# Batch 1's local attention heads in the transposed form and one slot earlier, with V loads and output buffers rearranged

## The chip, the cores and the metric

The kernel runs on one core of a Trainium2 chip. The metric is device time in microseconds (us) for one launch; the times shown are the median of several runs. A profile is of one execution, which has its own time; its span runs from the first to the last instruction.

## The reference

Sparse attention over 8 batches, 8 heads, 576 positions and head size 64, followed by a bilinear feed-forward layer:

```python
scores = scale * np.matmul(q, k.transpose(0, 1, 3, 2))
mask_local = (rel >= 0) & (rel < stride)                      # heads 0 to 3, stride 32
mask_strided = (rel >= 0) & (pos[None, :] % stride == pos[:, None] % stride)   # heads 4 to 7
attn = softmax(where(mask, scores, -1e9)); o = attn @ v
x = o.transpose(0, 2, 1, 3).reshape(B * S, H * D)             # 4608 x 512
out = ((x @ w_a) * (x @ w_b)) @ w_out                         # w_a, w_b: 512 x 1536; w_out: 1536 x 512
```

## The kernel before, in words

**Stages and slots.** The attention of batch 0 is written out by hand in a list (ORDER, L506). After it the kernel walks through 144 slots (L833): the feed-forward layer has 9 tiles of 512 tokens, and each tile has 16 slots. In slots 0 to 11 of a tile `ffn_ab` (L548) forms one block of 128 columns of x @ w_a and x @ w_b: eight matmuls at L545, a copy of the first result by ScalarE (L562), a product by VectorE into the tile `pf` (L565 or L567). In slots 12 to 15 the output is formed: for tiles 0, 1 and 2 by `ffn_y` (L692, twelve matmuls at L699, a copy by ScalarE at L705, a store by SyncE at L707, which the change calls plain outputs), for the later ones by `ffn_ys`. Slot numbers below count from the start, so slot 16 is the first of tile 1.

**Attention steps.** The attention of batches 1 to 7 is put between these matmuls. A unit `u` is a pair of heads (`c = u // 2`) and one half of the positions; units 0 to 3 are local heads, 4 to 7 strided ones. The steps are Tk and Tq (transposes of k and q by TensorE, batches 0 and 1 only), S (scores at L356, exponential by ScalarE at L364, mask by VectorE at L374), V (attention times V) and X (transposes of the result into `xT`, L479 and L495). The tables STEPS and LATER say behind which slot a step is issued; a position x.5 means in the middle of slot x + 1, after half of its matmuls. "V0(1)" below means step V of unit 0 of batch 1.

**Two forms of V.** Batches 0 and 1 use `V_p`, `V_r`, `V_n` (L383 to L433): the probabilities are the weights, V with one column of ones moves, so the output has positions on partitions and carries the sums; VectorE takes a reciprocal (L418) and multiplies (L433), and step X transposes. From batch `FIRST_D = 2` on, `step_VT` (L443) takes V and 64 columns of ones as the weights, and the probabilities move (L454): the output is already transposed and the sums lie on partitions 64 to 127. ScalarE takes the logarithm of the sums (L463) and the exponential of its negative (L464), and VectorE multiplies twice (L468 or L470), straight into `xT`. No X step is needed. The 64 columns of ones have to be in the V buffers before: `fill_v` (L109) writes them by a memset on GpSimd.

**Buffers and queues.** The V buffers `vl_buf` (local) and `vs_buf` (strided) are two each, used by batches of even and odd number. Each of the engines runs its own instructions in the order written; nothing is reordered by a scheduler. GpSimd (POOL) issues all loads from DRAM, one after another, through eight completion lanes: the load that takes a lane first waits until the load before it in that lane has landed. POOL also does memsets, and from slot 14 on a copy of one element (`pace`, L842) of the slot's result, which holds POOL's queue back to the slot whose loads come next. SyncE (SP) issues the stores of the outputs and, from batch 2 on, the copies from SBUF to SBUF that bring transposed k and q into place (L314, L318), issued by `step_D` (L292) behind transposes by VectorE (L299, L304). `do(i, f)` (L797) puts a piece of work behind slot i; the numbers `gs` (L811) say where the pieces of `step_D` go.

**Shared resources near the change.** PSUM has one buffer `o` for results of V after batch 0, one `st` for scores, one `tp` for transposes and three `mm`. The tile `y_sb` for plain outputs has two buffers, so the copy of output j waits for the store of output j - 2.

Of the kernel before, what the change touches and what calls it, by code (L numbers as in the profile page):

```python
# [7 lines left out]
F32 = mybir.dt.float32  # L8
# [6 lines left out]
FIRST_D = 2  # L15
# [15 lines left out]
def kernel(  # L31
# [10 lines left out]
    nc = tc.nc  # L42
    B, H, S, D = q.shape
    assert (B, H, S, D) == (8, 8, 576, 64)
    scale = 1.0 / (D ** 0.5)
    d_model = H * D
# [6 lines left out]
    HL = H // 2  # L53
# [6 lines left out]
    fsb = ctx.enter_context(tc.tile_pool(name="ffn", bufs=2))  # L60
# [21 lines left out]
    vl_buf = [const.tile([128, HL * 6, VW], BF16, name=f"vl{i}") for i in range(2)]  # L82
# [3 lines left out]
    vs_buf = [const.tile([NP, HL, RS, VW], BF16, name=f"vs{i}") for i in range(2)]  # L86
# [11 lines left out]
    def consts(i):  # L98
        if i == 0:
            for p in p_buf:  # L100
                nc.vector.memset(p[:, :, W:], 0.0)
        nc.vector.memset(kT_buf[i][0][:, :, 0:PAD], 0.0)
        nc.vector.memset(kT_buf[i][1], 0.0)
        nc.vector.memset(vl_buf[i][:, :, D:D + 1], 1.0)
        nc.vector.memset(vs_buf[i][:, :, :, D:D + 1], 1.0)
        if i == 0:
            nc.vector.memset(vl_buf[0][:PAD, 0, 0:D], 0.0)
# [44 lines left out]
    def spin(n):  # L152
        for _ in range(n):
            nc.tensor.matmul(cur["misc"][:, :224], lhsT=nc.const_aps.tensor(1.0, [128, 128], BF16),
                             rhs=nc.const_aps.tensor(1.0, [128, 224], BF16), start=True, stop=True)
# [58 lines left out]
    def load_vl(b, blocks=(0, HL * 6)):  # L214

        t = vl_buf[b % 2]
        f, e = blocks
        if (b, f) == (0, 0):
            f = 1
        src = bass.AP(tensor=v.tensor, offset=(b * H * S + LW * f - PAD) * D,  # L220
                      ap=[[D, 128], [LW * D, e - f], [1, D]])
        nc.gpsimd.dma_start(out=t[:, f:e, 0:D], in_=src)
# [17 lines left out]
    def load_w(c):  # L240
        f = slice(128 * WCH[c], 128 * WCH[c + 1])
        for src, dst in ((moe_w_a, wa_sb), (moe_w_b, wb_sb)):
            nc.gpsimd.dma_start(out=dst[:, :, f], in_=src.rearrange("(ko ki) f -> ki ko f", ki=128)[:, :, f])

    def load_wo(c):
        nc.gpsimd.dma_start(
            out=wo_sb[:, 3 * c:3 * (c + 1)],
            in_=moe_w_out.rearrange("(fo fi) d -> fi fo d", fi=128)[:, 3 * c:3 * (c + 1)],
        )
# [165 lines left out]
    def V_r(b, u):  # L415
        c, half, M, n, G = unit(u)
        rc = sb.tile([128, 2, 4], F32, tag="rc", name="rc")
        nc.vector.reciprocal(rc[:n, :, :G].unsqueeze(3), held[b, "o", u][1])  # L418
        held[b, "rc", u] = rc
# [13 lines left out]
        nc.vector.tensor_mul(dst, ov, rc[:n, :, :G].unsqueeze(3).to_broadcast([n, 2, G, D]))  # L433

    def step_V(b, u):
        if b >= FIRST_D:
            step_VT(b, u)
            return
        V_p(b, u)
        V_r(b, u)  # L440
        V_n(b, u)
# [55 lines left out]
    def step_X(b, c):  # L497
# [12 lines left out]
        F1b F1c""".split()  # L510


    STEPS = {1: {5: "Tk2", 5.5: "Tk3", 6: "Tq2", 7: "S4", 7.5: "Tq3", 8: "S5", 8.5: "V4", 9: "S6 Tk0", 9.5: "V5", 10: "S7 Tq0",
                 10.5: "V6", 11: "S0 Tk1", 11.5: "V7", 12: "Tq1 S1", 12.5: "V0 X2", 13: "S2", 13.5: "V1 X3 S3", 14: "V2",
                 14.5: "V3 X0", 15: "X1"},
             2: {20: "S0", 20.5: "S1", 21.5: "V0", 22: "S2", 23: "V1", 23.5: "S3", 24.5: "V2", 25: "S4", 26: "V3", 26.5: "S5",
                 27.5: "V4", 28: "S6", 28.5: "V5", 29: "S7", 29.5: "V6", 30: "V7"}}
    LATER = {-1: "S0", 0: "S1", 1: "V0", 2: "S2", 3: "V1", 4: "S3", 5: "V2", 6: "S4", 7: "V3", 8: "S5", 9: "V4", 10: "S6",
             11: "V5", 12: "S7", 12.5: "V6", 14: "V7"}
    FN = {"Tk": step_Tk, "Tq": step_Tq, "S": step_S, "V": step_V, "X": step_X}  # L520
# [10 lines left out]
    def mm_bank(shape):  # L531
        nm = "tp" if used[0] % 4 == 3 and used[0] >= 0 else "mm"
        used[0] += 1
        return psum4[nm].tile(shape, F32, tag=nm, name="mm")
# [50 lines left out]
    yst = {}  # L585
# [106 lines left out]
    def ffn_y(t, j, mid):  # L692
        pf = pfs[t]

        c0 = 0
        for z, n in enumerate((256, 128, 128) if (t, j) == (NT - 1, 3) else (d_model,)):
            y = mm_bank([128, n])
            for f in range(FD):
                nc.tensor.matmul(y, lhsT=pf[:, f, 128 * j:128 * (j + 1)], rhs=wo_sb[:, f, c0:c0 + n],  # L699
                                 start=(f == 0), stop=(f == FD - 1))  # L700
                if f == FD // 2 - 1:
                    mid()
            y_sb = fsb.tile([128, n], F32, tag="y_sb", name="y_sb", bufs=2)
            act = t < NT - 1 or (j + z) % 2 == 1
            (nc.scalar.copy if act else nc.vector.tensor_copy)(y_sb, y)  # L705
            r0 = TTOK * t + 128 * j
            (nc.scalar if z == 2 else nc.sync).dma_start(out=out[r0:r0 + 128, c0:c0 + n], in_=y_sb)  # L707
            c0 += n
        return y_sb[:1, :1]


    with tc.manual_schedule(engines={ENG.PE, ENG.SP, ENG.Pool, ENG.DVE, ENG.Activation}):
# [29 lines left out]
        for nm in ORDER:  # L742
            if nm[0] == "*":
                spin(int(nm[1:]))
            elif nm == "C0":
                for x, cp, n in ((raw[0], nc.vector.tensor_copy, "k"), (raw[1], nc.scalar.copy, "q")):
                    cp(nats[0, n, False][:, 0:2].rearrange("p h r d -> p (h r d)"), x[:96])
            elif nm == "C1":
                for p in (slice(PAD, 64), slice(64, 128)):
                    nc.vector.tensor_copy(vl_buf[0][p, 0, 0:D], raw[2][p, :D])  # L750
            elif nm == "M":
                mask_local2()
            elif nm[0] == "G":
                mask_group(int(nm[1]))
                if nm == "G1":
                    load_vs(0)
                    for c in range(2):
                        load_w(c)
                    load_w(2)
                    load_qk(1, True)  # L760
                    load_vs(1)
                    load_w(3)
                    load_qk(1, False)
                    load_w(4)
                    for c in range(4):
                        load_wo(c)
                    load_vl(1)
            elif nm == "Z":
                zero_qz(1, nc.scalar, ((0, 0),))
            elif nm[0] == "F":  # L770
                f = int(nm[1])
                if nm[2] == "a":
                    if f == 0:
                        ab = pst.tile([128, 2, 512], F32, tag="st", name="ab")
                        first[f] = [ab[:, 0], ab[:, 1]]
                    else:
                        first[f] = [psum4[x].tile([128, 512], F32, tag=x, name="ab") for x in ("misc", "o")]
                ab_mm(0, f, first[f], {"a": (0, 1), "b": (2,), "c": (3,)}[nm[2]])
            else:
                PART[nm[:-2] + nm[-1]](int(nm[-2]))  # L780
# [6 lines left out]
        for b in range(1, B):  # L787
            for pos, names in (STEPS.get(b) or {16 * (b - 1) + x: n for x, n in LATER.items()}).items():
                steps.setdefault(pos, []).append((b, names.split()))
# [7 lines left out]
        def do(i, fn, *args):  # L797
            at.setdefault(i, []).append(lambda: fn(*args))

        for b in range(FIRST_D, B):  # L800
            g0 = 16 * (b - 2)
            if b == FIRST_D:
                for g, fn, *a in ((0, load_qk, b, False), (1, load_qk, b, True), (3, load_vl, b), (6, load_vs, b)):
                    do(g0 + g, fn, *a)
            else:
                for h in range(HL):
                    do(g0 + h - (0 if b == FIRST_D + 1 else 2), load_qk, b, False, (h,))
                    do(g0 + h + (6 if b == FIRST_D + 1 else 2), load_qk, b, True, (h,))
                    do(g0 + h + 10, load_vs, b, (h,))
                do(g0 + (10 if b == FIRST_D + 1 else 7), load_vl, b)  # L810
            gs = {2: (14, 14, 14, 15, 16, 16, 17, 17, 18, 18), 3: (8, 9, 10, 11, 12, 13, 14, 15, 16, 17)}.get(b) or (  # L811
                3, 5, 7, 9, 12, 13, 14, 15, 16, 17)
            for (z, nm, part), g in zip(((0, "k", 0), (0, "k", 1), (0, "q", 0), (0, "q", 1), (1, "k", 0), (1, "k", 1),
                                         (1, "k", 2), (1, "q", 0), (1, "q", 1), (1, "q", 2)), gs):
                do(g0 + g, step_D, b, z, nm, part)
# [5 lines left out]
        for i, jz in ((2, (0, 0)), (3, (1, 0)), (0, (0, 1)), (5, (1, 1))):  # L821
            do(i, zero_qz, 0, nc.vector, (jz,))
        do(17, rezero, 1)
        for i, t in ((0, vl_buf[0]), (0, vs_buf[0]), (18, vl_buf[1]), (19, vs_buf[1])):
            do(i, fill_v, t)
        for n in range(5):
            for z in range(2):
                do(33 + 2 * n + z, fast_w, n, slice(3 * z, 3 * z + 3))
# [45 lines left out]
```

The softmax here doesn't subtract the row's maximum and nothing guards it: scores larger than these inputs give would overflow.

## Time and profile before

| | |
|---|---|
| median of 6 runs | 340.56 us (338.43 to 343.27) |
| the profiled execution | 338.43 us |
| its span | 336.3 us |
| TensorE matmuls busy | 323.6 us (96% of the span) |
| VectorE, ScalarE, GpSimd busy | 252.0, 202.2, 174.7 us |
| granted TensorE clock, mean | 0.995 |

The profiled execution is the fastest of the six; the rest of its time, 338.43 less 336.3, lies outside the span. PE's busy time overlaps: matmuls are pipelined, so the time that a matmul costs is the distance between the starts of two groups and not the duration in the row.

### The profile page before, as it was taken

How to read it: one execution, taken by the hardware profiler on the slowest of the kernel's cores; microseconds unless marked ns; L12 is line 12 of the kernel's file. 1: busy time of each engine (PE TensorE's matmuls, PEld its weight loads, DVE VectorE, ACT ScalarE, POOL GpSimd, SP SyncE). 2: the span in 40 equal slices, each digit the busy share in tenths (PEclk: the TensorE clock that was granted, in tenths of full speed). 3: DMA queues.
4: the chain of work that ended last, by engine and by line, in shares of the span. 5: the costliest groups of instructions: out<-in, count | busy, mean ns of one | idle time of the engine just before them, and what ended most of it. 6: DMA issues, size and time to landing. Idle time of an engine off the chain costs nothing.

```text
span 336.3 us, 7611 instructions
## 1 busy us (share of the span) xinstructions
PE 323.6 (96%) x2781; PEld 201.9 (60%) x2814; DVE 252.0 (75%) x475; ACT 202.2 (60%) x326; POOL 174.7 (52%) x293
## 2 busy tenths in 40 slices
PE   8999999999979999999999999999999999999992
PEld 6654555445535554556899985558555854674472
DVE  6867656758749984799999999999878744734561
ACT  5764855468758765787577756885678533223320
POOL 8934539899636644664577557843312031312132
PEclk9999999999999999999999999999999999999997
DMA  9999999998989699978898999899023022004004
GB/s 157 154 202 196 202 178 164 194 154 94 142 147 133 119 80 167 120 136 66 85 75 140 173 106 74 135 163 124 23 64 121 2 66 61 1 7 121 0 2 125
DMA packets 102446, 37.60 MB, mean 112 GB/s; under 512 B 77449, under 2 KB 98313, under 8 KB 102409
## 3 DMA queue, kind: packets, MB, share of 16 engines
q0 software_dynamic: 87760, 19.58, 64.8%
q1 hardware_dynamic: 14648, 17.53, 18.1%
q8 instruction: 22, 0.36, 0.4%
q14 instruction: 16, 0.12, 0.1%
HBM read 39.71 MB, written 9.44 MB: 146 GB/s over the span
## 4 chain that ended last, share of the span: by engine, by line
PE 68%; DMA 15%; POOL 6%; DVE 4%; issue 3%; ACT 1%; SPq 0%; DVEq 0%; ACTq 0%; POOLq 0%
PE mm L545 43%; PE mm L670 16%; DMA vl<-in_v_dram 4%; PE o L454 3%; DMA wa_sb<-in_moe_w_a_dram 3%; DMA shared<-in_k_dram 3%; PE st L356 3%; PE mm L699 3%; DMA qz10l<-tq 2%; DMA raw<-in_q_dram 1%; POOL vs L110 1%; POOL vl L110 1%; DMA natk<-in_k_dram 1%; DVE tq L299 1%; DMA out_dram<-y_sb 1%
## 5 line engine op out<-in xcount | busy, mean ns | idle before, releaser
L545 PE MATMUL mm<-xT,wa_sb 128*128 128x512 bf16 (+1 forms) x453 | 108.8, 357 | 1.5 <-DVE xT L470 0.6
L545 PE MATMUL mm<-xT,wb_sb 128*128 128x512 bf16 (+1 forms) x463 | 108.5, 357 | 0.3
L562 ACT COPY a_sb<-mm 128x512 f32<-128x512 f32 x106 | 62.1, 586 | 48.6 <-PE mm L545 46.4
L545 PEld LDWEIGHTS <-wb_sb 128*128 128x128 bf16 x480 | 46.4, 98 | 45.2 <-issue 1.5
L842 POOL CAST pace<-pf 1x1 f32<-1x1 bf16 x83 | 29.3, 353 | 82.5 <-DVE pf L565 73.7
L565 DVE TENSOR_TENSOR pf<-a_sb,mm 128x512 bf16<-128x512 f32 x72 | 48.5, 674 | 21.0 <-PE mm L545 17.9
L545 PEld LDWEIGHTS <-wa_sb 128*128 128x128 bf16 x480 | 42.6, 98 | 31.2
L364 ACT ACTIVATE p<-st 128x576 bf16<-128x576 f32 (+1 forms) x64 | 41.6, 650 | 10.1 <-PE st L356 9.5
L463 ACT ACTIVATE xr<-o 64x576 f32<-64x576 f32 x48 | 31.1, 647 | 24.8 <-PE o L454 24.5
L670 PEld LDWEIGHTS <-ps 128*128 128x128 bf16 x366 | 34.5, 98 | 5.3 <-DVE ps L578 1.2
L699 PE MATMUL mm<-wo_sb,pf 128*128 128x512 bf16 x140 | 33.7, 379 | 0.5 <-DMA wo_sb<-in_moe_w_out_dram 0.2
L464 ACT ACTIVATE xr<-xr 64x576 f32<-64x576 f32 x48 | 32.8, 683 | 1.5
L470 DVE TENSOR_TENSOR xT<-o,xr 64x288 bf16<-64x288 f32 x48 | 21.5, 448 | 14.8 <-ACT xr L464 13.8
L567 DVE TENSOR_TENSOR pf<-a_sb,mm 128x512 bf16<-128x512 f32 x34 | 22.9, 674 | 7.6 <-ACT a_sb L562 5.7
L468 DVE TENSOR_TENSOR xT<-o,xr 64x288 bf16<-64x288 f32 x48 | 21.5, 448 | 9.0 <-ACT xr L464 8.4
L670 PE MATMUL mm<-wf,ps 128*128 128x256 bf16 x210 | 26.3, 273 | 0.1
L374 DVE TENSOR_TENSOR p<-p,mask_l 128x576 int16<-128x576 int16 x32 | 19.4, 607 | 7.5 <-ACT p L364 7.5
L234 POOL DMA_DIRECT2D vs<-in_v_dram x24 | 19.5, 816 | 5.0 <-PE st L356 2.8
L699 PEld LDWEIGHTS <-pf 128*128 128x128 bf16 x144 | 12.9, 98 | 13.4 <-issue 0.5
L842 POOL COPY pace<-y_sb 1x1 f32<-1x1 f32 x18 | 3.4, 187 | 33.6 <-ACT y_sb L626 14.8
L210 POOL DMA_DIRECT2D ql<-in_q_dram x24 | 16.0, 665 | 7.1 <-DMA wo_sb<-in_moe_w_out_dram 3.7
L210 POOL DMA_DIRECT2D kl<-in_k_dram x24 | 16.0, 668 | 5.8 <-issue 3.5
(137 smaller groups left out, 479.5 us busy)
## 6 DMA issues: line engine op xcount, KB each, us to landing
out_dram<-y_sb SPq DMA_DIRECT2D x32, 256.0 KB
vl<-in_v_dram POOLq DMA_DIRECT2D x7, 384.0 KB, 8.9
kl<-in_k_dram POOLq DMA_DIRECT2D x24, 72.0 KB, 3.0
ql<-in_q_dram POOLq DMA_DIRECT2D x24, 72.0 KB, 3.2
vs<-in_v_dram POOLq DMA_DIRECT2D x24, 72.0 KB, 4.6
wo_sb<-in_moe_w_out_dram POOLq DMA_DIRECT2D x4, 384.0 KB, 11.4
natk<-in_k_dram POOLq DMA_DIRECT2D x20, 72.0 KB, 3.0
natq<-in_q_dram POOLq DMA_DIRECT2D x20, 72.0 KB, 3.2
```

The costliest lines, as they stand in the source:

```text
L210: nc.gpsimd.dma_start(out=t[32 * h:32 * h + 32], in_=src[b, h].rearrange("(i y) d -> y i d", y=32))
L364: nc.scalar.activation(p[:M, :, :W], st[:M, :, :W], ACT.Exp, scale=scale)
L463: nc.scalar.activation(r, sums, ACT.Ln)
L464: nc.scalar.activation(r, r, ACT.Exp, scale=-1.0)
L468: nc.vector.tensor_mul(dst[:, W * half:W * (half + 1)], o[:64, j, :W], r[:, j])
L545: nc.tensor.matmul(ps_[:, c0:c0 + n], lhsT=w[:, kk, 128 * f:128 * (f + 1)], rhs=xT[:, kk, x0:x0 + n], start=(kk == first and c0 == 0), sto ...
L562: nc.scalar.copy(a_sb, ab[0])
L565: nc.vector.tensor_mul(pf[:, f, :].rearrange("p (i a s) -> p a i s", i=2, s=16), halves(a_sb), halves(ab[1]))
L567: nc.vector.tensor_mul(pf[:, f, :], a_sb, ab[1])
L670: nc.tensor.matmul(dst, lhsT=lhs(g, q), rhs=rhs(g)[:, n], start=g == 0 and (tail and k == "7" or new and q == 0), stop=g == FG - 1, skip_g ...
L699: nc.tensor.matmul(y, lhsT=pf[:, f, 128 * j:128 * (j + 1)], rhs=wo_sb[:, f, c0:c0 + n], start=(f == 0), stop=(f == FD - 1))
L842: nc.gpsimd.tensor_copy(pace, done)
```

## The change

In four parts:

1. Units 0 to 3 of batch 1 (the local heads) use `step_VT`. Their steps X0 and X1 go. The steps of batch 1 are moved: V follows its S by about one slot instead of one and a half, V0(1) moves from the middle of slot 13 to the middle of slot 12, V3(1) stays in the middle of slot 15. The strided units 4 to 7 keep their form.
2. `vl_buf[1]` has to hold 64 columns of ones before batch 1, so the fills are moved to slot 0 (`vl_buf[1]`, `vl_buf[0]`, `vs_buf[0]`), and the loads of the last chunk of w_a and w_b, of w_out and of batch 1's local V are moved from ORDER to slot 0, between the fills. The order of the loads among themselves stays. The small memset of ones for `vl_buf[1]` on VectorE goes.
3. Batch 2's loads of V are issued behind slot 16 (local) and slots 18 to 21 (one strided head each) instead of slots 3 and 6, where POOL had issued them behind the loads of batch 2's k and q. The transposes of batch 2's local k go from slot 14 to slot 13, one of its local q from slot 15 to 14, one piece of its strided k from slot 16 to 15. V7(2) moves from behind slot 30 to the middle of slot 31.
4. A plain output takes half of a tile of 128 x 2 x 512: two outputs share a tile, and there are two tiles. The size of the tag in SBUF stays, since the later tiles' outputs use it in this size already.

```diff
-        nc.vector.memset(vl_buf[i][:, :, D:D + 1], 1.0)
+        if i == 0:
+            nc.vector.memset(vl_buf[i][:, :, D:D + 1], 1.0)
...
     def step_V(b, u):
-        if b >= FIRST_D:
+        if b >= FIRST_D or u < 4:
             step_VT(b, u)
             return
...
-    STEPS = {1: {5: "Tk2", 5.5: "Tk3", 6: "Tq2", 7: "S4", 7.5: "Tq3", 8: "S5", 8.5: "V4", 9: "S6 Tk0", 9.5: "V5", 10: "S7 Tq0",
-                 10.5: "V6", 11: "S0 Tk1", 11.5: "V7", 12: "Tq1 S1", 12.5: "V0 X2", 13: "S2", 13.5: "V1 X3 S3", 14: "V2",
-                 14.5: "V3 X0", 15: "X1"},
+    STEPS = {1: {5: "Tk2", 5.5: "Tk3", 6: "Tq2", 7: "S4", 7.5: "Tq3", 8: "V4 S5", 8.5: "Tk0", 9: "V5 S6", 9.5: "Tq0",
+                 10: "V6 S7", 10.5: "S0", 11: "V7 Tk1", 11.5: "V0 S1", 12: "Tq1", 12.5: "V1 S2", 13: "X2 S3", 13.5: "V2 X3",
+                 14.5: "V3"},
              2: {20: "S0", 20.5: "S1", 21.5: "V0", 22: "S2", 23: "V1", 23.5: "S3", 24.5: "V2", 25: "S4", 26: "V3", 26.5: "S5",
-                 27.5: "V4", 28: "S6", 28.5: "V5", 29: "S7", 29.5: "V6", 30: "V7"}}
+                 27.5: "V4", 28: "S6", 28.5: "V5", 29: "S7", 29.5: "V6", 30.5: "V7"}}
...
-            y_sb = fsb.tile([128, n], F32, tag="y_sb", name="y_sb", bufs=2)
+            if j % 2 == 0:
+                yst[t] = fsb.tile([128, 2, d_model], F32, tag="y_sb", name="y_sb", bufs=2)
+            y_sb = yst[t][:, j % 2, :n]
...
                     load_qk(1, False)
-                    load_w(4)
-                    for c in range(4):
-                        load_wo(c)
-                    load_vl(1)
...
+        do(0, fill_v, vl_buf[1])
+        do(0, load_w, 4)
+        do(0, fill_v, vl_buf[0])
+        for c in range(4):
+            do(0, load_wo, c)
+        do(0, load_vl, 1)
+        do(0, fill_v, vs_buf[0])
         for b in range(FIRST_D, B):
             g0 = 16 * (b - 2)
             if b == FIRST_D:
-                for g, fn, *a in ((0, load_qk, b, False), (1, load_qk, b, True), (3, load_vl, b), (6, load_vs, b)):
-                    do(g0 + g, fn, *a)
+                do(0, load_qk, b, False)
+                do(1, load_qk, b, True)
+                do(16, load_vl, b)
+                for h in range(HL):
+                    do(18 + h, load_vs, b, (h,))
...
-            gs = {2: (14, 14, 14, 15, 16, 16, 17, 17, 18, 18), 3: (8, 9, 10, 11, 12, 13, 14, 15, 16, 17)}.get(b) or (
+            gs = {2: (13, 13, 14, 14, 15, 16, 17, 17, 18, 18), 3: (8, 9, 10, 11, 12, 13, 14, 15, 16, 17)}.get(b) or (
...
-        for i, t in ((0, vl_buf[0]), (0, vs_buf[0]), (18, vl_buf[1]), (19, vs_buf[1])):
-            do(i, fill_v, t)
+        do(19, fill_v, vs_buf[1])
```

## The prediction

> **What bounds the kernel now.** I read the table by stages first: PE is busy 96% of the span, and from 104 us on it lacks under 1 us in each 30, so nothing there can be won but by fewer matmuls. The idle time that the change can touch lies before 104 us. The timeline of PE shows it, gap by gap (start, us, work, and in brackets the idle time before it and what ended it):
>
> ```profile
> 46.27 0.41 PE L410 MATMUL o<-vs,p 72*128 72x65 bf16 x8
> ...
> 47.53 0.81 PE L699 MATMUL mm<-wo_sb,pf 128*128 128x512 bf16 x3 [0.20 <-DMA wo_sb<-in_moe_w_out_dram]
> ...
> 50.21 0.35 PE L410 MATMUL o<-vl,p 128*128 128x65 bf16 x6
> ...
> 59.38 0.30 PE L479 MATMUL tp<-ident,xr 96*128 96x96 bf16 x3 [0.38 <-DVE xr L433]
> ...
> 69.04 0.22 PE L356 MATMUL st<-qz01l,kT0l 128*128 128x96 bf16 x1 [0.57 <-DMA qz01l<-tq]
> ...
> 94.04 0.43 PE L454 MATMUL o<-p,vs 72*128 72x72 bf16 x8 [1.10 <-DVE xT L470]
> ...
> 99.20 0.38 PE L545 MATMUL mm<-xT,wa_sb 128*128 128x512 bf16 x1 [0.59 <-DVE xT L470]
> ```
>
> The last two waits have one cause, seen on ScalarE: a plain output's copy waits for the store of two outputs before, and V7(2)'s logarithm stands behind it.
>
> ```profile
> 92.35 0.68 ACT L464 ACTIVATE xr<-xr 64x576 f32<-64x576 f32 x1
> 96.23 0.59 ACT L705 COPY y_sb<-mm 128x512 f32<-128x512 f32 x1 [3.20 <-DMA out_dram<-y_sb]
> 96.84 0.65 ACT L463 ACTIVATE xr<-o 64x576 f32<-64x576 f32 x1
> ```
>
> What no wait on PE shows is how close a transfer comes. The chain of waits in order of time has batch 1's local V:
>
> ```profile
> 35.74 0.93 issue
> 36.67 13.38 DMA vl<-in_v_dram
> 50.05 0.28 issue
> 50.33 0.66 POOL ql L210
> ```
>
> It lands at 50.05, and V0(1), its first user, starts on PE at 50.21: it fits by 0.16 us. So the row speaks against calling V0 sooner.
>
> **The change part by part.**
>
> **Work on PE.** Distances between starts: six matmuls of the old V take 0.18 us (55.50 to 55.68), of the new one 0.25 (72.14 to 72.39), an X of six 0.25 (57.16 to 57.41). Four V cost 4 x 0.07 = +0.28, two X save 0.50: -0.22. ScalarE gets four pairs of 0.65 + 0.68 and loses two copies of 0.64 (+4.0); VectorE gets eight multiplies of 0.45 and loses four pairs of 0.19 + 0.55 (+0.6). The two are busy 5.4 and 6.3 of the 9.3 us from 50.2 to 59.5, so it fits as a sum; the order is looked at below.
>
> **V0(1) one slot sooner.** The middle of slot 12, where V0(1) now stands, is where V7(1) stands in the trace: 46.27. It ends 0.25 later, so PE asks for `vl` at about 46.5. Slots 8 to 11 may cost up to 0.7 before that (V5 now stands one slot behind S5, and VectorE does the two instructions of V4, 0.2 + 0.7, ahead of S5's mask); the wait below swallows it. The load is not sooner: it stays behind the same loads of w and w_out, and its place in POOL is held by the lane (1.37 us idle before 36.67, for batch 1's k). The two fills ahead (1.40 us each by the row of the memset at 50.98) go into idle time of 1.48 us before 29.37 and, for the second, of 0.19 + 1.37 us before 36.67. w_out is issued 1.4 us later, but at 32.1 the loads of w ahead of it are still running (the last lands at 40.1), so the queue doesn't run dry. I leave the landing at 50.05, with 1 us to either side, as the mixing of w_out with `vl` isn't shown.
>
> Here the Trainium skill ("DMA: Bandwidth & Descriptors", section "Anatomy of one DMA") weighs the other way: a load from the GpSimd queue takes about 2.0 us plus its bytes over 436 GB/s. For 384 KB that is 2.9 us; `vl` would be there at 39.6, before 46.5, and this step would cost nothing. The row has 13.38 for this very load, behind a queue of w and w_out. I take the row.
>
> PE then goes from V0(1) at 50.13 by the new order: 4 V x 0.25, 3 S x 0.26, Tq1 0.38, 2 X x 0.25, seven halves of an output at 1.30 and slot 16 (1.73): 13.5 us. One new wait: Tq1 moves next to S2. ScalarE, after V0 (start to end of both activations 1.84 by 72.14 to 73.98), has S1's exponential (0.54), output 0's copy (0.48) and q's two copies (2 x 0.64): ready at 54.3, while PE wants S2's second matmul at 53.9; with 0.1 at S3 that is 0.5. V3's product is ready at 63.6 and slot 16 asks for that chunk of `xT` at 63.7: nothing. So slot 17 starts at 50.1 + 13.5 + 0.5 = 64.1, against 61.26 before (last matmul at 61.04 plus 0.22): **+2.85 us**. This already holds the -0.22 and the ends of the waits of 0.20 and 0.38. Bounds: +1.8 to +3.9, by the landing.
>
> **Batch 2's V loads behind the query transfers.** In 59.5 to 72.1 the queues are full (DMA share 1.96 by the table of stages), and S0(2) waits 0.57 us for q. With 3072 + 4 x 576 short rows gone from there, q is in place about 1 us sooner relative to S0(2): **-0.57** (0 to -0.57). What it risks: `vl` is issued behind slot 16's pace: 64.1, plus copy, product and pace, 1.5: at 65.6. V0(2) asks at 64.1 + 4 slots of 1.73 + S0 0.26 + 2.86 (69.26 to 72.14) = 74.2, that is 8.6 us later. The median from issue to landing is 8.9 for these loads (page), 5.5 to 14.0 with all nine; batch 2's own took 9.1 (58.46 to 67.60) behind eight loads that are now through. I take +0.1 here (0 to 5.4, weighed below). Moved past POOL's queue: the four strided heads (0.82 each, 3.3) now stand among batch 3's loads, the memset of `vl_buf[1]` (1.4) is gone from there, so batch 3's k and q are issued some 1.9 us later relative to PE. At slot 24 VectorE's first transpose of k ran at 79.01 with 0.43 us until the multiply behind it was due (80.15): I add +0.2 (0 to 1). The fill of `vs_buf[0]` (1.83) stands before k and q of batch 2, in time that POOL spent waiting for lanes (four times 1.2 us from 40.8 to 47.8).
>
> **Four half buffers, V7(2) half a slot later.** Output 2 of tile 1 now waits for stores of tile 0, done 25 us before. The 3.20 us on ScalarE go. V7(2) has the 1.30 us of six more matmuls between it and V6(2): its wait of 1.10 for `o` goes. Its product is then ready 2.65 us after its start (0.25 + 0.65 + 0.68 + 0.91 and handovers), and the chunk of `xT` is asked for after 0.25 + 1.30 + 0.26 + 1.30 = 3.1: the 0.59 goes too, with some 0.15 around it. **-1.8** (-0.5 to -1.9: S0(3) now comes 1.1 us sooner, and its q has to have landed; the transfer issued at 87.96 took 5.92). In tile 2 PE is busy 7.95 of 8 us from 128 to 136: nothing there. What is left out: the memset of `vl_buf[1]`'s ones (0.08, early, hidden).
>
> **Sum.** 2.85 - 0.57 + 0.1 + 0.2 - 1.8 = **+0.8 us** on the span, 336.3 to 337.1; the profiled execution 338.43 would be 339.2. That one is the fastest of six, the median lies 2.1 above it; the same step on the median gives 340.56 + 0.8 = **341.3**.
>
> **The rivals.**
>
> *The load is there in time.* If `vl` lands before about 47.2 (mixed in the queue with a w_out that starts later), the 2.9 us of waiting vanish; S2's wait stays: 341.3 - 2.6 = 338.7. For it: w_out is issued 1.4 later. Against it: w_out's chunks land 1.9 us apart at some 200 GB/s, so the queue is bound by bytes, and the same bytes stand ahead.
>
> *The end's gain doesn't come* (an engine off the path): q of batch 3 is late at S0(3), or POOL's later loads put VectorE behind at slots 24 to 28; then -1.8 becomes about 0 and one more wait of 0.5 comes: 341.3 + 2.3 = 343.6. For it: the V loads of batch 3 lie on top of those transfers. Against: they did before, and start 1.9 us later now.
>
> *Slower, by one wait:* batch 2's local V at slot 16. With 14.0 us, the worst row, V0(2) waits 5.4: 346.6. With the -0.57 it is a loss on the whole from 8.0 us on; it goes beyond 1% when the landing takes about 11.3 us. For it: the load that took 13.38 us. Against: nothing of w is in the queue any more.
>
> *The change does nothing to the path*, as all of it is hidden: 340.6. Against it stand the 0.16 us of slack and the wait on ScalarE.
>
> **How the numbers follow.** Forecast 0.57; load in time 0.12; no gain at the end 0.17; late V of batch 2 0.10; nothing 0.04. A measurement of this kernel can tell about 1% from no change, 3.4 us: 337.2 and 344.0 are the marks. Faster: of the load in time (338.7, with 1 us of scatter) 0.05 and of the forecast's tail 0.02: 0.07. Slower: of late V 0.08, of no gain at the end 0.06, of the forecast 0.03: 0.17. The rest, 0.76, is within. The range from 338.7 (the load in time) to 344.1 (no gain at the end, with a landing 0.5 later) leaves out some 2 in 10. The forecast's own range is 339.5 to 342.8, from its terms' bounds.
>
> **What would show it.** Right: on PE a wait of about 3 us before the first `o<-p,vl` near 50, ended by the load; slot 17's first matmul near 64; no copy on ScalarE that waits for a store near 95, no waits at V7(2) and slot 32, nothing at S0(2). Wrong: if V0(1) starts at 47 without a wait, the queue's order isn't what I think; if V0(2) waits over 1 us, the load behind slot 16 is the price; if PE has waits in 8 to 11 that aren't swallowed, the distance of one slot from S to V is too short.

## The result, and the profile after

| | before | after |
|---|---|---|
| median | 340.19 us (72 runs, 338.43 to 344.14) | 339.47 us (35 runs, 338.22 to 341.27) |
| ratio after to before | | 0.998, 95% interval 0.9967 to 0.9993 |
| profiled execution, device time | 338.43 us | 338.91 us |
| mean granted TensorE clock | 0.995 | 0.995 |

The forecast was 341.3 us, a loss of 0.8. By the medians it is a gain of 0.7, small but beyond its interval; by the two profiled executions it is a loss of 0.5. Both are true: the profiled execution of before was the fastest of all 72 runs of that kernel. Device times are compared below and not spans: the last product of VectorE moved by +0.43 us (it starts at 330.46 in place of 330.03) and the device time by +0.48, while the span moved by 0.9, since the part of the device time that lies outside of it differs between the two kernels (1.7 and 2.1 us). The 35 runs of the changed kernel fall into two groups with nothing between them, 21 from 338.22 to 339.53 us and 14 from 340.22 to 341.27 us, the latter at a mean granted clock of 0.979 to 0.993; the profiled execution is of the first kind, and the clock is taken up at the end.

TensorE (PE) in its timeline, after (start, us, work, and in brackets the idle time before it; lines of the code have moved by up to three):

```profile
40.60 0.42 PE L411 MATMUL o<-vs,p 72*128 72x65 bf16 x8 [0.92 <-DVE p L375]
...
46.42 0.42 PE L411 MATMUL o<-vs,p 72*128 72x65 bf16 x8
...
47.15 1.47 PE L700 MATMUL mm<-wo_sb,pf 128*128 128x512 bf16 x6
50.36 0.41 PE L455 MATMUL o<-p,vl 128*128 128x96 bf16 x6 [1.74 <-issue]
...
54.56 0.20 PE L357 MATMUL st<-qz11l,kT1l 128*128 128x96 bf16 x1 [0.16 <-ACT qz11l L289]
...
96.52 0.42 PE L455 MATMUL o<-p,vs 72*128 72x72 bf16 x8
```

The row at 50.36 is V0(1), at the place that the forecast gave it (50.13) and behind a wait. The row names "issue" and not the load, but GpSimd's queue shows when the load landed: it is issued at 36.72, and the next load that takes its lane goes out at 50.55.

```profile
36.72 1.47 POOL L223 DMA_DIRECT2D vl<-in_v_dram  x1 [0.63 <-issue]
...
50.55 0.66 POOL L211 DMA_DIRECT2D ql<-in_q_dram  x1 [1.90 <-DMA vl<-in_v_dram]
...
66.46 1.46 POOL L223 DMA_DIRECT2D vl<-in_v_dram  x1 [0.29 <-issue]
```

So batch 1's V was there by 50.36, about 13.6 us after its issue (13.38 before); that V0(1) waits for it is shown below by a kernel that issues it sooner. The Trainium skill's price that the prediction set beside it ("DMA: Bandwidth & Descriptors", "Anatomy of one DMA", 2.9 us as an estimate) is again wrong for this load, behind this queue. The last line is batch 2's local V, behind slot 16: V0(2) uses it at 74.59, without a wait.

On ScalarE the copy of a plain output no longer waits for a store:

```profile
94.81 0.68 ACT L465 ACTIVATE xr<-xr 64x576 f32<-64x576 f32 x1
95.51 0.59 ACT L708 COPY y_sb<-mm 128x512 f32<-128x512 f32 x1
...
96.98 0.65 ACT L464 ACTIVATE xr<-o 64x576 f32<-64x576 f32 x1 [0.88 <-PE o L455]
```

The copy starts 0.02 us after the exponential ahead of it; before, it stood 3.20 us idle there. What this gives on PE is seen in the table by stages. Its columns are: stretch and its length; busy us and instructions of PE, PE's weight load, VectorE, ScalarE, GpSimd; granted clock; DMA share; GB/s. Before:

```profile
88.00:104.00 16.00, 14.21 (x111) 7.36 (x111) 9.18 (x19) 10.45 (x17) 7.41 (x16) 1.00 1.27 162
```

After:

```profile
88.00:104.00 16.00, 15.89 (x122) 8.27 (x123) 11.33 (x22) 12.38 (x21) 11.11 (x22) 1.00 1.58 185
```

PE's idle time in these 16 us fell from 1.79 to 0.11 us, with the waits at V7(2) and slot 32. From V6(2) to batch 3's V0 the changed kernel takes 8.37 us (93.67 to 102.04) where before takes 10.40 (91.21 to 101.61), so these two executions give 2.0 us for part 4. More than that was lost around 50 us: slot 17 starts at about 64.55 in place of 61.26.

### The profile page after: what moved, and what is told of

Same layout as the page of the kernel before. It is cut to its first block, busy times and chain, and to the rows that moved or that the text cites. A ratio compares the mean times of both kernels' runs of the same rounds, so it can differ in the third digit from the quotient of the medians.

```text
span 337.2 us, 7599 instructions
## 1 busy us (share of the span) xinstructions
PE 323.4 (96%) x2769; PEld 201.7 (60%) x2802; DVE 253.2 (75%) x474; ACT 205.9 (61%) x332; POOL 174.9 (52%) x295
## 3 DMA queue, kind: packets, MB, share of 16 engines
q0 software_dynamic: 87760, 19.58, 64.1%
## 4 chain that ended last, share of the span: by engine, by line
PE 88%; ACT 3%; POOL 2%; issue 2%; DMA 2%; DVE 2%; POOLq 0%; DVEq 0%; ACTq 0%
PE mm L546 52%; PE mm L671 16%; PE mm L700 9%; PE st L357 4%; PE o L455 4%; DMA vl<-in_v_dram 2%; POOL shared L196 1%; PE o L411 1%; PE ab L546 1%; ACT a_sb L563 1%; DVE pf L568 0%; PE tp L480 0%; ACT qz11l L289 0%; ACT p L365 0%; POOL pace L850 0%
## 5 line engine op out<-in xcount | busy, mean ns | idle before, releaser
L464 ACT ACTIVATE xr<-o 64x576 f32<-64x576 f32 x52 | 33.7, 647 | 31.0 <-PE o L455 30.1
L469 DVE TENSOR_TENSOR xT<-o,xr 64x288 bf16<-64x288 f32 x56 | 25.0, 447 | 15.4 <-ACT xr L465 14.8
L465 ACT ACTIVATE xr<-xr 64x576 f32<-64x576 f32 x52 | 35.5, 683 | 1.7
L471 DVE TENSOR_TENSOR xT<-o,xr 64x288 bf16<-64x288 f32 x48 | 21.5, 448 | 11.1 <-ACT xr L465 10.3
```

The lines of the kernel that those rows point to most:

```text
L464: nc.scalar.activation(r, sums, ACT.Ln)
L465: nc.scalar.activation(r, r, ACT.Exp, scale=-1.0)
L469: nc.vector.tensor_mul(dst[:, W * half:W * (half + 1)], o[:64, j, :W], r[:, j])
```

## The experiments

Each kernel was timed beside before on one chip. The change in us is the ratio, less 1, times the median of before in that comparison.

| kernel | median, us | ratio (95% interval) | change, us |
|---|---|---|---|
| before again | 339.65 | 1.0013 (0.9989 to 1.0037) | +0.4 |
| parts 1 and 2 alone | 341.71 | 1.0061 (1.0032 to 1.0090) | +2.1 |
| part 3's loads alone | 342.55 | 1.0066 (1.0048 to 1.0084) | +2.2 |
| part 4 alone, with V7(2) | 337.13 | 0.9914 (0.9886 to 0.9941) | -2.9 |
| the change without part 4 | 346.61 | 1.0185 (1.0147 to 1.0222) | +6.3 |
| the change without part 3's loads | 339.36 | 0.9980 (0.9963 to 0.9998) | -0.7 |
| the change, batch 1's V ahead of w_out | 337.88 | 0.9937 (0.9919 to 0.9954) | -2.1 |
| half buffers alone | 338.82 | 0.9967 (0.9949 to 0.9986) | -1.1 |
| V7(2) later alone | 340.79 | 1.0022 (1.0000 to 1.0044) | +0.7 |
| before without batch 3's V loads | 339.18 | 0.9990 (0.9958 to 1.0021) | -0.3 |
| parts 3 and 4 | 337.95 | 0.9932 (0.9908 to 0.9957) | -2.3 |
| part 3's loads alone, without batch 3's V loads | 338.48 | 0.9932 (0.9900 to 0.9964) | -2.3 |

V7(2)'s move, listed under part 3 above, is tried with part 4. The earlier transposes of part 3 stay in "parts 1 and 2 alone" and in "the change without part 3's loads"; they are missing in "part 3's loads alone" and "parts 3 and 4". They were not tried by themselves.

### The parts one by one

My theory was the prediction's: V0(1)'s early place costs over 2 us, the half buffers give 1.8, part 3's loads give some tenths. The rivals were that one of the parts acts only together with another.

**Before, unchanged.** No edit.

> The kernel before once more, unchanged; a second profile of it. The theory (the profiled execution of before, 338.43 us, was its luckiest, with short waits before 104 us, and the median one, 1.7 us longer, waits longer for transfers there): PE's idle time from 40 to 104 us is 4.5 us or more where the first profile had some 3.5, at the same clock, and the time is near 340. The rival (the waits are the same in each execution and the rest is the clock): idle time within 0.4 us of the first profile, and a time above 339.5 goes with a mean granted clock below 0.995. Ratio 1.000 either way.

It gave 1.0013, with no difference. The profiled execution (338.51 us) was again one of the fastest, so it doesn't decide between the two. It has the same waits in other sizes: 3.34 us at the store, 0.73 at slot 32, 0.48 at S0(2).

**Parts 1 and 2 alone.** From the changed kernel:

```diff
-27.5: "V4", 28: "S6", 28.5: "V5", 29: "S7", 29.5: "V6", 30.5: "V7"}}
+27.5: "V4", 28: "S6", 28.5: "V5", 29: "S7", 29.5: "V6", 30: "V7"}}
...
-            if j % 2 == 0:
-                yst[t] = fsb.tile([128, 2, d_model], F32, tag="y_sb", name="y_sb", bufs=2)
-            y_sb = yst[t][:, j % 2, :n]
+            y_sb = fsb.tile([128, n], F32, tag="y_sb", name="y_sb", bufs=2)
...
-                do(0, load_qk, b, False)
-                do(1, load_qk, b, True)
-                do(16, load_vl, b)
-                for h in range(HL):
-                    do(18 + h, load_vs, b, (h,))
+                for g, fn, *a in ((0, load_qk, b, False), (1, load_qk, b, True), (3, load_vl, b), (6, load_vs, b)):
+                    do(g0 + g, fn, *a)
```

> Batch 1's local heads with V and ones as weights, the new order of batch 1's steps and of the fills; the V loads of batch 2, the output tiles and V7(2) as before. The prediction's sum: V0(1) waits for its V to about 50.1, slot 17 starts 2.9 to 3.3 us later than in before, the time is +2.3 to +2.9 (the 0.57 at S0(2) may go or stay), ratio 1.007 to 1.009. The rival (before's median execution already waits there for the same load, or has other waits there that this form doesn't have): +1.5 or less, ratio at most 1.0045, with the wait at V0(1) still in the profile.

It cost 2.1 us, a little under the 2.3 to 2.9 expected. V0(1) starts at 50.29, after 2.58 us of waiting, and in this kernel no wait is left at S0(2), though batch 2's V loads stand where they stood: the last copy of q goes out at 69.61, 3.27 us ahead of S0(2) at 72.88, where in before it is 0.76 (67.51 and 68.27). PE comes later, and this kernel has part 3's earlier transposes too; which of the two gives q its lead isn't separated. The profile, at 342.17 us, holds a cost that the prediction doesn't have: after the wait the granted clock falls to 0.50 for some 3.4 us (see the end), which is 1.7 us lost.

**Part 3's loads alone.** From before:

```diff
-                for g, fn, *a in ((0, load_qk, b, False), (1, load_qk, b, True), (3, load_vl, b), (6, load_vs, b)):
-                    do(g0 + g, fn, *a)
+                do(0, load_qk, b, False)
+                do(1, load_qk, b, True)
+                do(16, load_vl, b)
+                for h in range(HL):
+                    do(18 + h, load_vs, b, (h,))
```

> Only batch 2's loads of V behind slots 16 and 18 to 21, on the kernel before. The prediction's sum: -0.57 for the wait at S0(2), +0.1 at V0(2), +0.2 by POOL's later loads: -0.3, ratio 0.999. The theory of the lucky profile: S0(2) waits longer in the median execution of before, so -1 to -2, ratio 0.994 to 0.997. The rival that this part costs: V0(2) waits over 1 us for the load, +0.5 or more.

The forecast of -0.3 fell. S0(2)'s wait is gone, as said, and yet it is 2.2 us slower. The loss is on ScalarE, on PE at slot 32 and in SyncE's (SP's) queue, in this order:

```profile
98.78 0.58 ACT L705 COPY y_sb<-mm 128x512 f32<-128x512 f32 x1 [5.60 <-PE mm L545]
```

```profile
101.75 0.38 PE L545 MATMUL mm<-xT,wa_sb 128*128 128x512 bf16 x1 [2.99 <-DVE xT L470]
```

```profile
93.44 6.29 SPq L707 DMA_DIRECT2D out_dram<-y_sb  x3
```

The copy of output 2 waits 5.60 us in place of 3.20. The releaser in its row is PE, long done: the copy goes on when output 0's store has landed. That store is issued at 93.44 and the copy goes on at 98.78, 5.3 us later; in before the same distance is 2.3 us (93.94 to 96.23). In this kernel GpSimd issues batch 3's V loads from 87.27 to 92.5, up to 3 us later than before, where the first one goes out at 84.23. Whether those loads delay the store is tried below.

**Part 4 alone**, the half buffers and V7(2) half a slot later, from before:

```diff
-27.5: "V4", 28: "S6", 28.5: "V5", 29: "S7", 29.5: "V6", 30: "V7"}}
+27.5: "V4", 28: "S6", 28.5: "V5", 29: "S7", 29.5: "V6", 30.5: "V7"}}
...
-            y_sb = fsb.tile([128, n], F32, tag="y_sb", name="y_sb", bufs=2)
+            if j % 2 == 0:
+                yst[t] = fsb.tile([128, 2, d_model], F32, tag="y_sb", name="y_sb", bufs=2)
+            y_sb = yst[t][:, j % 2, :n]
```

> Only the four half output tiles and V7(2) half a slot later, on the kernel before. The prediction's sum: -1.8, ratio 0.9947, both waits (1.10 and 0.59) near 94 and 99 us gone. The theory of the lucky profile: more than the sum, -2.3 to -3.5, ratio 0.990 to 0.993, since the median execution has a longer wait of ScalarE for the store than 3.20 us. If ratio is above 0.997 the end's gain doesn't come and something else takes it.

It gave 2.9 us (interval 2.0 to 3.9), more than the 1.9 that the prediction allowed at most, and in the middle of the 2.3 to 3.5 expected if the profile's waits were short ones. It has the lowest median measured here, under both kernels of the case (338.22 us is the fastest run of the changed one). Its stages:

```profile
88.00:104.00 16.00, 16.00 (x124) 8.37 (x123) 11.30 (x23) 12.00 (x20) 8.65 (x17) 1.00 1.50 177
```

PE has no idle time left from 88 to 104 us; in before it was 1.79.

### What each part does inside the change

**The change without part 4.**

```diff
-            if j % 2 == 0:
-                yst[t] = fsb.tile([128, 2, d_model], F32, tag="y_sb", name="y_sb", bufs=2)
-            y_sb = yst[t][:, j % 2, :n]
+            y_sb = fsb.tile([128, n], F32, tag="y_sb", name="y_sb", bufs=2)
...
-27.5: "V4", 28: "S6", 28.5: "V5", 29: "S7", 29.5: "V6", 30.5: "V7"}}
+27.5: "V4", 28: "S6", 28.5: "V5", 29: "S7", 29.5: "V6", 30: "V7"}}
```

> The changed kernel with two whole output tiles again and V7(2) behind slot 30. The prediction's sum had the store's wait at 3.2 us on ScalarE, worth 1.8 on PE whatever else is changed: the time would be before's +2.6, ratio 1.0075. The theory after the first runs (POOL issues batch 3's V loads later when batch 2's stand behind slot 16, they then lie on the stores of tile 1, and the half tiles are what makes this harmless): +4 to +6 against before, ratio 1.012 to 1.018, and a wait of 5 us or more of ScalarE for the store in the profile.

+6.3 us: a little above the end of what was expected. Its profiled execution (349.47 us, clock 0.971) began late, so only its waits near 100 us are read: the copy of output 2 waits 5.28 us for the store, and PE 2.67 at slot 32 and 1.1 at V7(2); here too the clock then falls to 0.50 (109.2 to 112.6). The parts alone add up to 2.1 + 2.2 = 4.3. The other 2.0 us aren't placed; the mean clock of its runs is low, 0.971 to 0.990, and how much of them that is was not tried.

**The change without part 3's loads.**

```diff
-                do(0, load_qk, b, False)
-                do(1, load_qk, b, True)
-                do(16, load_vl, b)
-                for h in range(HL):
-                    do(18 + h, load_vs, b, (h,))
+                for g, fn, *a in ((0, load_qk, b, False), (1, load_qk, b, True), (3, load_vl, b), (6, load_vs, b)):
+                    do(g0 + g, fn, *a)
```

> The changed kernel with batch 2's V loads behind slots 3 and 6 again. The prediction's sum: the wait at S0(2) is back, +0.57 less 0.3, so before's +1.1 or about 341. The theory after the first runs: with half tiles the V loads' place costs and brings little; between 338.8 and 340.2, ratio 0.997 to 1.001 against before, S0(2) waiting at most 0.6. The rival (part 3 pays in the changed kernel): 340.5 or more.

0.998, the same as the change itself. Part 3's loads bring nothing in this kernel, and cost nothing. In its profile (340.73 us) V0(1) waits 2.25 us, and the clock falls behind it.

**Batch 1's local V ahead of w_out.**

```diff
         do(0, load_w, 4)
+        do(0, load_vl, 1)
         do(0, fill_v, vl_buf[0])
         for c in range(4):
             do(0, load_wo, c)
-        do(0, load_vl, 1)
```

> The changed kernel with the load of batch 1's local V ahead of the four loads of w_out in POOL's order, the fill of the first V buffer between them. The theory that V0(1) waits for the place of its load: the wait of 1.9 us at V0(1) goes, 0.4 comes back as a wait of tile 0's first output for w_out's last quarter; -1.2 to -1.9 against the changed kernel, 337.6 to 338.3, ratio 0.993 to 0.995 against before. The rival (the order in the queue doesn't set the landing, all loads share the engines): V lands near 50 us again and the time stays at 339.5.

0.9937, or 1.5 us below the change (337.88 against 339.36 without part 3's loads in the same comparison, and 339.47). V0(1) has no wait, and a short one for w_out comes in its place:

```profile
48.54 0.42 PE L455 MATMUL o<-p,vl 128*128 128x96 bf16 x6
...
50.48 0.81 PE L700 MATMUL mm<-wo_sb,pf 128*128 128x512 bf16 x3 [0.62 <-DMA wo_sb<-in_moe_w_out_dram]
```

Of what parts 1 and 2 cost, then, the landing of this one load is about 1.5 us net, with what its wait does to the clock in part of the executions. V5's wait of 0.92 stays, in slot 9, where V5 now stands one slot behind S5.

**Before, a third profile.** No edit.

> The kernel before, a third profile. If it is an execution above 339.3 us: by the theory of the lucky profile, ScalarE waits for the store longer than 3.3 us near 95 us; by the rival, the wait is the same and the clock lower.

339.12 us, with 3.54 at the store and 0.94 at slot 32: a longer wait, in an execution just short of the 339.3 us named.

### Where part 4's gain comes from

**Half buffers alone.**

```diff
-            y_sb = fsb.tile([128, n], F32, tag="y_sb", name="y_sb", bufs=2)
+            if j % 2 == 0:
+                yst[t] = fsb.tile([128, 2, d_model], F32, tag="y_sb", name="y_sb", bufs=2)
+            y_sb = yst[t][:, j % 2, :n]
```

> The kernel before with the four half output tiles alone; V7(2) stays behind slot 30. From the profile of before: ScalarE's wait of 3.2 us for the store goes and with it the 0.59 (and some 0.15) at slot 32, the 1.10 at V7(2) stays: -0.75, ratio 0.998. The theory that before's median execution waits longer for the store than its profiled ones: -1.5 to -2.2, ratio 0.9935 to 0.9955.

-1.1 us (-0.5 to -1.7): slot 32's wait is gone, V7(2)'s 1.10 for the one `o` buffer stays. The size lies between the two that were set against each other, -0.75 and -1.5 to -2.2, and is what the mean wait of six profiles of before gives (0.96 + 0.15, below).

**V7(2) later alone.**

```diff
-27.5: "V4", 28: "S6", 28.5: "V5", 29: "S7", 29.5: "V6", 30: "V7"}}
+27.5: "V4", 28: "S6", 28.5: "V5", 29: "S7", 29.5: "V6", 30.5: "V7"}}
```

> The kernel before with V7(2) in the middle of slot 31 alone; two whole output tiles. The wait of 1.10 for o at V7(2) goes, but the logarithm of V7(2) still stands behind the copy that waits for the store, so slot 32 asks 1.1 us sooner for the same late product: 0 (-0.3 to +0.1), ratio 0.999 to 1.000. If it gives -1.1 by itself (ratio 0.997), the two waits add and the store's has no part in V7(2)'s.

Nothing, or a little loss (0 to +1.5 us), where -0.3 to +0.1 was expected. V7(2)'s wait goes, and slot 32 gets it back:

```profile
101.15 0.38 PE L545 MATMUL mm<-xT,wa_sb 128*128 128x512 bf16 x1 [1.95 <-DVE xT L470]
```

The copy still waits 3.28 us for the store, so V7(2)'s product comes as late as ever, and PE only waits for it at another place. Of the two edits of part 4 one is worth 1.1 us alone and the other nothing; together they remove both waits and give 2.9.

**Before without batch 3's V loads.** Batch 3 multiplies with batch 1's V here. A rival theory of mine was that the store in before is slow as those loads run beside it.

```diff
-                    do(g0 + h + 10, load_vs, b, (h,))
-                do(g0 + (10 if b == FIRST_D + 1 else 7), load_vl, b)
+                    if b > FIRST_D + 1:
+                        do(g0 + h + 10, load_vs, b, (h,))
+                if b > FIRST_D + 1:
+                    do(g0 + 7, load_vl, b)
```

> The kernel before without the five loads of batch 3's V; batch 3 multiplies with batch 1's V instead, all instructions of the engines stay. The theory that the store near 95 us is late because these loads' packets lie on the same DMA engines: ScalarE's wait for the store falls from 3.2 us to 1.5 or less, slot 32's wait goes, -0.7 in the profile and -1.5 to -2.2 in the median, ratio 0.9935 to 0.9955. The rival (the store is late only because SP issues it behind ten copies of q and k): the wait stays above 2.5 us and the ratio above 0.998.

That theory fell: 0.999 (no difference within its interval, -1.4 to +0.7 us), and the copy still waits 2.98 us. In before the store is late since it is issued late. Output 0's copy on ScalarE, and SyncE's queue, in before:

```profile
86.83 0.59 ACT L705 COPY y_sb<-mm 128x512 f32<-128x512 f32 x1
```

```profile
86.73 0.54 SPq L318 DMA_DIRECT2D qz10l<-tq  x1
...
93.16 0.59 SPq L318 DMA_DIRECT2D qz11l<-tq  x1
93.94 3.23 SPq L707 DMA_DIRECT2D out_dram<-y_sb  x3
```

Output 0 lies in its buffer from 87.42, and its store is issued at 93.94, behind ten copies of batch 3's q and k, of which each holds the queue for about 0.6 us (those that wait for a transpose, longer). The row counts three stores in a group; its 3.23 us holds the third one's wait for its own copy.

**Parts 3 and 4**: the edits of part 3's loads and of part 4 from above, on before.

> The kernel before with the half tiles, V7(2) later and batch 2's V loads behind slots 16 to 21; batch 1's local heads as before. With the half tiles in place, part 3's cost (2.2 us alone) should vanish and its gain at S0(2), 0.4 in the profile with part 4 alone, should show: -0.2 to -0.5 against part 4 alone, 336.6 to 336.9, ratio 0.990 to 0.991. If part 3 costs by something else than the store (V0(2) late, POOL's later loads), 337.6 or more.

0.9932, no better than part 4 alone (0.9914; the intervals overlap), and at 337.95 us beyond the 337.6 from which part 3 was said to cost by something else than the store. Its one profile (340.76 us, the longest of ten runs) shows such a cost. VectorE stands 2.31 us idle for one of SyncE's copies of q, the multiply behind it comes late, and V6(2) on PE waits for that:

```profile
93.82 0.71 DVE L304 STREAM_TRANSPOSE tk<-natk 128x512 bf16<-128x512 bf16 x1 [2.31 <-DMA qz10l<-tq]
```

```profile
95.47 0.42 PE L454 MATMUL o<-p,vs 72*128 72x72 bf16 x8 [1.00 <-DVE xT L470]
```

In part 4 alone neither is there. So in this execution the half buffers make part 3's loads harmless at the store, but not at these copies.

**Part 3's loads alone, without batch 3's V loads**: the edits of part 3's loads and of the kernel just above; batch 3 multiplies with batch 1's V again.

> Part 3 alone as before, and batch 3's V loads left out in addition (batch 3 multiplies with batch 1's V, so its result differs). Theory (part 3 alone costs +2.2 because batch 3's V loads then run at the same time as tile 1's first store): without them the store of output 0 lands about 2.3 to 3 us after its issue as in the kernel before instead of 5.3, the copy of output 2 waits about 3 us instead of 5.6, and the median comes down by 1.5 to 2.5, to about the kernel before (ratio 0.996 to 1.002). Rival (the longer wait comes from the later place of SyncE's copies of q and k, or from the V loads of batch 2 themselves): the wait stays at 5 or more and the ratio stays near 1.0066.

On the store and the wait it held; the median came down by more than the 1.5 to 2.5 us said. ScalarE and SyncE of this kernel:

```profile
96.99 0.59 ACT L705 COPY y_sb<-mm 128x512 f32<-128x512 f32 x1 [3.18 <-DMA out_dram<-y_sb]
```

```profile
94.67 3.26 SPq L707 DMA_DIRECT2D out_dram<-y_sb  x3
```

The store lands 2.3 us after its issue again (94.67 to 96.99), the wait is 3.18, and the ratio falls from 1.0066 to 0.9932, by 4.5 us. The same loads that are harmless in before, where they are issued up to 3 us sooner, cost that when they run together with the store. On PE's waits 3.0 us of it are seen (slot 32 2.99 in place of 0.57, and 0.56 at the row of V6(2), at 91.37). In the profiles the rest is the clock. Behind slot 32's long wait eight matmuls of part 3's loads alone go at half speed:

```profile
102.44 1.91 PE L545 MATMUL mm<-xT,wa_sb 128*128 128x512 bf16 x4
104.14 1.87 PE L545 MATMUL mm<-xT,wb_sb 128*128 128x512 bf16 x4
```

The same eight without batch 3's V loads:

```profile
100.64 1.03 PE L545 MATMUL mm<-xT,wa_sb 128*128 128x512 bf16 x4
101.50 1.03 PE L545 MATMUL mm<-xT,wb_sb 128*128 128x512 bf16 x4
```

From start to start it is 1.70 us in place of 0.86, so the two groups cost 1.7 us more; 3.0 + 1.7 = 4.7 stands against the measured 4.5.

### How far one profile of before can be trusted

Part 4 gave more than its waits in the first profile of before could. To see whether that profile is typical, before was profiled three more times and part 4 once.

> The kernel before, one more profiled execution. By the theory that its executions differ in the store's wait: one above 339.5 us at a clock of 0.994 or more shows ScalarE waiting 3.8 us or more near 95 us and slot 32 waiting 1.2 us or more; by the rival, the time is lost in the first 20 us (late first loads) or in no wait at all, and the store's wait stays at 3.2 to 3.5.

> As before_p1: the kernel before, another profiled execution. The theory wants the store's wait to grow with the time of the execution, by about as much; the rival wants it unchanged.

> As before_p1: the kernel before, another profiled execution. The theory wants the store's wait to grow with the time of the execution, by about as much; the rival wants it unchanged.

> Part 4 alone once more. Both theories: no wait of ScalarE for a store near 95 us, no wait at V7(2) and slot 32. The time is within 0.6 us of 337.1 unless the first loads come late, which then shows as idle time of PE before 20 us.

| before, profiled execution | device time, us | wait for the store | slot 32 | S0(2) |
|---|---|---|---|---|
| the one of the prediction | 338.43 | 3.20 | 0.59 | 0.57 |
| second | 338.51 | 3.34 | 0.73 | 0.48 |
| third | 339.12 | 3.54 | 0.94 | 0.74 |
| fourth | 339.33 | 4.04 | 1.43 | 0.47 |
| fifth | 339.63 | 3.70 | 1.09 | 0.89 |
| sixth | 340.30 | 3.60 | 0.99 | 0.65 |

The fourth one, on ScalarE and on PE:

```profile
96.92 0.59 ACT L705 COPY y_sb<-mm 128x512 f32<-128x512 f32 x1 [4.04 <-PE mm L699]
```

```profile
99.89 0.38 PE L545 MATMUL mm<-xT,wa_sb 128*128 128x512 bf16 x1 [1.43 <-DVE xT L470]
```

The prediction's profile has the shortest wait for the store, the shortest at slot 32 and the shortest time. That the waits grow with the time, as the theory wanted, isn't so: the two executions above 339.5 us wait 3.70 and 3.60 us, less than the 3.8 that was named for them, and the longest wait is in the fourth. The mean at slot 32 is 0.96 us, 0.37 more than I put into the sum. V7(2)'s wait is 1.10 in each. Part 4's two profiles, without any of these waits at the store and slot 32, took 336.88 and 337.37 us, 2.1 below the mean of the six (339.22).

## Why the prediction was wrong

**The half buffers, the term that failed: "-1.8 (-0.5 to -1.9)".** Its mechanism was right in each step: no copy waits for a store, both waits on PE are gone. Its size was read from the waits of the fastest execution, and so was its upper end. With the mean waits of six profiles it is 1.10 + 0.96 + 0.15 = 2.2; by the medians it is 2.9 (2.0 to 3.9) alone, and inside the change the ratios 0.9980 / 1.0061 = 0.992 give about 2.8. With it failed the sentence that carried the sum over: "the same step on the median". The wait for the store is 3.64 us on average in the other five profiles, against 3.20 in the fastest, so removing it is worth more on the median. The 0.7 us between 2.2 and 2.9 lie within the interval, and their cause stays open; without them the change would be near zero (2.1 - 2.2) and not a gain of 0.7.

**V0(1) one slot sooner: "+2.85 (+1.8 to +3.9)".** Right in the profile. V0(1) starts at 50.36 (50.13 said), slot 17 at 64.55 (64.1 said), with slots 13 to 16 as counted. Its wait is 1.74 and not about 3.6, as PE comes to it at 48.45 and not at 46.5. Of these 1.95 us, 0.72 is a later start of this execution (slot 0's first matmul at 23.37 in place of 22.65), and 1.2 are slots 8 to 11, V5's 0.92 among them, for which I had allowed up to 0.7. The wait swallowed it all, as said. What the prediction left out is the clock behind this wait: this execution began late and waited 1.74 us at full clock, while parts 1 and 2 alone began at 22.48, waited 2.58 us and lost 1.7 us more at half clock. On runs with a mean clock of 0.994 or more alone, parts 1 and 2 cost 1.7 us (341.55 against 339.85) and part 4 gives 2.7 (337.13); so it is in part by luck that the medians' +2.1 meets the forecast so well.

**S0(2)'s wait: "-0.57".** It goes. Part 3's loads alone remove it, as said, but so do parts 1 and 2 with the earlier transposes, without these loads; in the change the loads aren't needed for it. The sum stays the same: 2.85 - 0.57 = +2.3 for that kernel, measured +2.1 (1.1 to 3.1).

**Part 3's later loads: "+0.1" and "+0.2".** Neither is seen in the change: V0(2) doesn't wait, and the change with and without these loads is at 0.998. What I missed is a rival: I asked what POOL's later queue does to k and q, and not what it runs beside. With two whole output buffers, the later V loads of batch 3 fall on tile 1's first store and cost over 2 us net by themselves. In the rival on batch 2's local V one sum is off: by its own terms (8.6 us, and 0.57 gained) the part turns into a loss when the landing takes about 9 us, and not 8.0. Nothing hangs on it, as the load is issued at 66.46 and V0(2) uses it at 74.59, 8.1 us later.

**Sum.** +2.1 - 2.9 + 0 = -0.8, measured -0.7 (-0.2 to -1.1). The prediction's sum was right for the two profiled executions (339.2 said, 338.91 measured) and wrong in sign for the medians. Of the rivals, "the load is there in time" didn't happen but was made to, by the load ahead of w_out: 337.88, where 338.7 was said. The others didn't come. That the sum fits the two profiled executions is partly luck: 0.72 us of late start in the changed one were swallowed by V0(1)'s wait, and its clock did not fall.

## What to carry to other kernels

Size a removed wait for a DMA from several executions, or at least state whether the profiled one is at the edge of the runs: here the fastest of six had the shortest wait for the store and the shortest behind it. Where a change makes TensorE wait in one long piece, read the granted clock behind that wait before calling the wait its whole price. A store that is issued from a queue with other transfers is late by what stands ahead of it, so ask for its issue time before blaming bandwidth, and give the buffer behind it another half before moving anything else. Try the parts of a change alone: here part 4 carried the whole gain, and parts 1 and 2 gave most of it back.

## What the runs showed of the hardware beyond that

**Colliding transfers.** The same V loads made no difference in before (0.999), and one of 4.5 us beside the same store when issued up to 3 us later (1.0066 against 0.9932), with nothing changed in their sizes: the time of issue decided. The store's landing went from 2.3 to 5.3 us. The table by stages shows it from 92 to 96 us, first for before, then for part 3's loads alone:

```profile
92.00:96.00 4.00, 2.90 (x21) 1.26 (x20) 1.08 (x3) 1.00 (x2) 0.00 (x0) 1.00 1.04 203
```

```profile
92.00:96.00 4.00, 2.90 (x22) 1.28 (x20) 1.23 (x3) 1.15 (x2) 0.50 (x1) 1.00 2.18 171
```

The DMA share (its next to last column) doubles from 1.04 to 2.18, while the bytes moved fall from 203 to 171 GB/s.

**The clock behind a long wait.** After waits of TensorE of 2.25 us (V0(1), the change without part 3's loads), 2.58 (V0(1), parts 1 and 2 alone), 2.67 (slot 32, the change without part 4) and 2.99 us (slot 32, part 3's loads alone) the granted clock, read in windows of half a us, falls to 0.50 for some 3.4 us; after 1.74 (the change) and 1.95 us (slot 32, V7(2) later alone) it stays at 1.00. The first of these, in windows of 1 us (the clock is the third number from the end):

```profile
50.68 0.42 PE L455 MATMUL o<-p,vl 128*128 128x96 bf16 x6 [2.25 <-issue]
```

```profile
52.00:53.00 1.00, 1.00 (x4) 0.15 (x1) 0.46 (x2) 0.97 (x2) 1.00 (x3) 0.50 1.50 96
53.00:54.00 1.00, 1.00 (x14) 0.64 (x14) 0.90 (x2) 0.87 (x3) 1.00 (x3) 0.50 1.25 160
```

Half a clock for 3.4 us is 1.7 us lost. It fits the 1.6 us between the medians of the two groups of the changed kernel's runs, though none of those at the lower clock was profiled. The length of the wait isn't the whole rule: three profiles (part 3's loads without batch 3's V loads, parts 3 and 4, the change without part 4) also have half a clock before 28 us, where the longest wait is 1.89 us, and in one of them it lasts 13 us; what sets it there isn't shown.

**First loads.** Executions of one unchanged kernel differ in their first loads: from the first to the sixth profile of before, slot 0's first matmul moves from 22.65 to 23.22 and the wait for w_out grows from 0.20 to 0.73; together that is 1.1 of the 1.9 us between them, before any of the places that the change touches.
